# Routing of attention output to experts: one piece per pair of batches, or small steps beside attention blocks

## The chip, the cores and the metric

The kernel runs on one core of a Trainium2 chip. The metric is the device time of one execution in microseconds (us), lower is better. The executions came from several chips; a ratio is always taken between kernels that ran in the same rounds on the same chip. An execution counts as fast when it is within 1.5% of the fastest of its kernel in those rounds, otherwise as slow. Each also has a mean granted clock of TensorE (PE), 1.0 being full speed.

## The reference

The first half is chunked attention over 4 batches, 8 heads, 768 tokens and 64 dims. Its output, with the heads joined to 512 columns, goes into a mixture of 8 experts. A token takes its own best expert if it is the first of its batch or if its local gate is under 0.5; otherwise it keeps the expert of the token before it, so a batch is a chain.

```python
for b in range(B):
    prev_e = -1
    for s in range(S):
        fresh_e = int(np.argmax(logits[b, s]))
        if s == 0 or local_gate[b, s] < 0.5:
            e = fresh_e
        else:
            e = prev_e if prev_e >= 0 else fresh_e
        prev_e = e
        p = softmax(logits[b, s])
        h = np.maximum(x[b, s] @ w1[e], 0.0)
        out[b, s] = p[e] * (h @ w2[e])
```

## The kernel before

Attention runs in 32 blocks of 96 queries (NB = 32, 8 to a batch, NR = 16 to a pair of batches, HALF = 4). Each block has, as the trace counts them, 16 score matmuls, 16 value matmuls, four transposes ("turn") and, every fourth block, a group of gate logits. After each pair of batches the rows are routed: VectorE (DVE) picks experts and runs the chain as scans, the place of every row is worked out, GpSimd (POOL) scatters the rows of x to DRAM, grouped by expert, and gathers them back as tiles of 128. The first pair is routed while the second pair's attention runs, and the first five tiles ("early") come from it alone. Weights come in 8 pieces of 512 KB a tile, so 16 for the first two tiles, issued by SyncE (SP), which issues the loads of q and k too; v is issued by ScalarE (ACT). Loads run three blocks ahead.

```python
xp = ctx.enter_context(tc.tile_pool(name="xp", bufs=3))     # x of one batch: 3 for 4 batches
ld = inner.enter_context(tc.tile_pool(name="ld", bufs=AHEAD + 1))   # AHEAD = 3

def load(n):
    qt = ld.tile([P, HP, QB], F32, name="qt")
    nc.sync.dma_start(qt, q[n])
    kt = ld.tile([P, HP, P], F32, name="kt")
    nc.sync.dma_start(kt, k[n])
    vt = ld.tile([P, H, VW], F32, name="vt")
    nc.scalar.dma_start(vt, v[n])
    return qt, kt, vt

# ... scores, values, turned, logits cut ...

def route_ranks():                       # after route_picks over all 16 blocks
    onehot = sm.tile([PE2, S], F32, name="onehot")
    for half in range(2):
        # 4 transposes of pick into c_ps, a copy of its second part to stays
        nc.vector.tensor_tensor_scan(
            onehot[:, HQ * half:HQ * half + HQ], stays, c_ps[0:PE2].rearrange("p j n -> p (j n)"),
            onehot[:, HQ - 1:HQ] if half else 0.0, ALU.mult, ALU.add)
    rank = sm.tile([PE2, S], F32, name="rank")
    nc.vector.tensor_tensor_scan(rank, onehot, onehot, 0.0, ALU.add, ALU.max)
    # ... count kept ...

def route_rows(r, x, ex, tot, rank):
    # transposes of rank to r_ps, row numbers and probabilities on DVE, then for b, n:
    ins = nc.gpsimd.indirect_dma_start(            # 16 scatters a pair
        out=x_dram[:, :], out_offset=bass.IndirectOffsetOnAxis(ap=row[:, i:i + 1], axis=0),
        in_=x[b][0:QB, n].bitcast(I32), in_offset=None).ins

for n in range(NB):
    b, j = divmod(n, NQB)
    if j == 0:
        xs[b] = xp.tile([P, NQB, XW], F32, name="x")
    ahead = begin(n + 1) if n + 1 < NB else None   # scores of the next block, load n + 4
    make_values(*begun, n, xs[b][0:QB, j])
    begun = ahead
    if n > 0:
        turn(n - 1)                                # transposes, every fourth time the logits
    if n == NR:
        held["picks"] = route_picks(lts.pop(0))
    if n == NR + 1:
        held["ranks"] = route_ranks()
    if n == NR + 2:
        route_places(*held["ranks"])
    if n == NR + 3:
        route_rows(0, (xs.pop(0), xs.pop(1)), *held["picks"], held["ranks"][1])
    if n == NR + 4:
        early, done = plan_early()
    if n == NR + 6:
        early_xs = [gathered(early, i, (0,)) for i in range(EARLY)]
        # ... the pieces of the first two tiles' weights ...
    if n >= NR + 6:
        next(pieces)                               # one weight piece a block
for _ in pieces:
    pass
turn(NB - 1)
# ... then the experts: per tile 64 matmuls h_ps, 16 matmuls y_ps ...
```

## Time and profile before

| | kernel before |
|---|---|
| time of its first three executions | 558.06, 570.56, 573.6 us |
| profiled execution | 557.94 us, span 556.1 us, mean clock 0.947 |
| PE at half clock before 200 us of the span | 87.31 to 128.27 and 141.92 to 145.33, 44.4 us |
| first expert matmul | 140.63 us |
| rest of the span | 415.5 us |

In each profile quoted below that isn't from the chip described under C, the span minus the start of the first expert matmul is 414.2 to 417.0 us.

The page's row of engines (busy us, share of the span, instructions) says who is busy:

```profile
PE 531.4 (96%) x3614; PEld 406.4 (73%) x3614; DVE 88.0 (16%) x323; ACT 111.8 (20%) x224; POOL 90.8 (16%) x112
```

PE is the bound; DVE and POOL have much room.

### The profile page before, as it was taken

Reading aid. Unit: us, or ns where it says so; the run is one execution under the profiler, and the core shown is the slowest. Engines: PE = TensorE matmul, PEld = TensorE weight load, DVE = VectorE, ACT = ScalarE, POOL = GpSimd, SP = SyncE. Lnnn points to the kernel's source line nnn. Section 1 sums busy time; section 2 is a strip of 40 time slices with the busy share of each in tenths; the row PEclk is TensorE's granted clock in tenths of the full one; section 3 lists DMA queues with packets and bytes.
Section 4 is the critical chain, followed back from the end, with each engine's and each line's share of the span. In section 5 each row is a group of like instructions: output and inputs, shape, how many; then the busy total and the mean of one; then the engine's idle time right before and its main releaser. Section 6 shows DMA issues by size and latency. Waiting matters only on the chain.

```text
span 556.1 us, 9356 instructions
## 1 busy us (share of the span) xinstructions
PE 531.4 (96%) x3614; PEld 406.4 (73%) x3614; DVE 88.0 (16%) x323; ACT 111.8 (20%) x224; POOL 90.8 (16%) x112
## 2 busy tenths in 40 slices
PE   8999999998999999999999999999999999999970
PEld 5888889896877777777777777777777777766640
DVE  4333474123333000000000000000000100000000
ACT  3555553233110111111111111111111111101010
POOL 2000017310027321111111111112222111000000
PEclk9999996558899999999999999999999999999995
DMA  8777769995889999888989898889999998880000
GB/s 299 241 212 215 214 205 292 354 354 225 321 323 352 362 406 353 334 328 323 326 324 325 328 332 324 318 323 339 343 345 335 342 330 325 316 322 26 21 7 3
DMA packets 52761, 158.00 MB, mean 284 GB/s; under 512 B 7707, under 2 KB 11805, under 8 KB 52704
## 3 DMA queue, kind: packets, MB, share of 16 engines
q1 hardware_dynamic: 40320, 127.94, 64.1%
q0 software_dynamic: 6720, 20.78, 9.8%
q10 hardware_dynamic: 5664, 8.54, 5.1%
q8 instruction: 33, 0.54, 0.4%
q14 instruction: 24, 0.20, 0.1%
HBM read 144.62 MB, written 13.40 MB: 284 GB/s over the span
## 4 chain that ended last, share of the span: by engine, by line
PE 87%; issue 6%; DMA 2%; DVE 1%; ACT 0%; POOL 0%; POOLq 0%; DVEq 0%; ACTq 0%
PE h_ps L619 31%; PE y_ps L629 30%; PE o_ps L236 10%; PE s_ps L224 7%; DMA out_dram<-y,to 2%; PE xt_ps L279 2%; PE g_ps L606 2%; PE lt_ps L288 1%; PE l_ps L294 1%; PE z_ps L124 1%; DVE rank L348 0%; PE c_ps L341 0%; DVE x L239 0%; DVE onehot L344 0%; POOL out_dram L632 0%
## 5 line engine op out<-in xcount | busy, mean ns | idle before, releaser
L619 PEld LDWEIGHTS h_ps<-gxt,w_sb 128*128 128x128 f32 x1728 | 198.5, 193 | 14.2 <-issue 9.8
L619 PE MATMUL h_ps<-gxt,w_sb 128*128 128x128 f32 x1728 | 200.1, 277 | 3.3 <-DVE gxt L608 2.5
L629 PE MATMUL y_ps<-w_sb,ht 128*128 128x512 f32 x432 | 189.9, 592 | 0.0
L629 PEld LDWEIGHTS y_ps<-w_sb,ht 128*128 128x128 f32 x432 | 80.0, 190 | 90.4 <-issue 89.4
L632 POOL DMA_INDIRECT out_dram<-y,to x27 | 27.4, 1015 | 336.0 <-ACT y L631 320.9
L621 ACT ACTIVATE ht<-h_ps 128x512 f32<-128x512 f32 x54 | 32.2, 597 | 165.4 <-PE h_ps L619 165.4
L236 PE MATMUL o_ps<-vt,pt 128*96 128x65 f32 x512 | 60.3, 275 | 0.3 <-ACT pt L229 0.3
L236 PEld LDWEIGHTS o_ps<-vt,pt 128*96 128x96 f32 x512 | 54.5, 187 | 4.3 <-issue 1.7
L631 ACT ACTIVATE y<-y_ps,xs 128x512 f32<-128x512 f32 x24 | 16.5, 687 | 160.9 <-PE y_ps L629 154.2
L224 PE MATMUL s_ps<-qt,kt 64*128 64x96 f32 x512 | 46.7, 316 | 0.0
L224 PEld LDWEIGHTS s_ps<-qt,kt 64*128 64x128 f32 x512 | 39.2, 217 | 10.1 <-issue 7.0
L384 POOL DMA_INDIRECT x_dram<-x,row x32 | 29.5, 921 | 89.4 <-DVE x L379 80.2
L610 DVE TENSOR_TENSOR to<-xs,past_late 128x1 int32<-128x1 f32 x19 | 3.0, 160 | 236.0 <-DMA xs<-x_dram,rows_late 236.0
L608 DVE COPY gxt<-g_ps 128x512 f32<-128x512 f32 x27 | 18.6, 688 | 92.8 <-PE g_ps L606 92.8
L229 ACT ACTIVATE pt<-s_ps,mask_mid 128x256 f32<-128x256 f32 x72 | 29.0, 472 | 15.0 <-PE s_ps L224 14.7
L239 DVE TENSOR_TENSOR x<-o_ps,rinvs 96x256 f32<-96x256 f32 x64 | 26.8, 418 | 1.7
L280 ACT COPY xt<-xt_ps 128x384 f32<-128x384 f32 x32 | 15.3, 477 | 34.6 <-PE xt_ps L279 34.6
L238 DVE RECIPROCAL rinvs<-o_ps 96x4 f32<-96x4 f32 x64 | 11.4, 177 | 65.1 <-PE o_ps L236 64.1
L496 POOL DMA_INDIRECT xs<-x_dram,rows_late x19 | 18.3, 963 | 12.5 <-DMA x_dram<-x,row 7.1
L279 PE MATMUL xt_ps<-ident,x 96*128 96x96 f32 x128 | 18.5, 274 | 0.3 <-DVE x L239 0.3
L279 PEld LDWEIGHTS xt_ps<-ident,x 96*128 96x128 f32 x128 | 14.7, 167 | 0.5 <-issue 0.5
L606 PE MATMUL g_ps<-ident,xs 128*128 128x128 f32 x96 | 14.6, 273 | 0.0
(168 smaller groups left out, 131.1 us busy)
## 6 DMA issues: line engine op xcount, KB each, us to landing
w_sb<-in_w_dram SPq DMA_DIRECT2D x216, 512.0 KB, 6.7
vt<-in_v_dram ACTq DMA_DIRECT2D x32, 260.0 KB, 3.6
kt<-in_k_dram SPq DMA_DIRECT2D x32, 256.0 KB, 3.6
qt<-in_q_dram SPq DMA_DIRECT2D x32, 192.0 KB, 3.3
x_dram<-x,row POOLq DMA_INDIRECT x32, 7.8
out_dram<-y,to POOLq DMA_INDIRECT x27, 7.9
xs<-x_dram,rows_late POOLq DMA_INDIRECT x19, 7.8
x<-x_dram,rows_late POOLq DMA_INDIRECT x7, 8.1
```

What stands on the lines that cost most here:

```text
L224: nc.tensor.matmul(st[:, u, a], lhsT=kt[h, a], rhs=qt[h, a], start=True, stop=True)
L229: nc.scalar.activation(pt[:, :, :, c], st[:, :, :, c], ACT.Exp, bias=m[:, g:g + 1], scale=SCALE)
L236: nc.tensor.matmul(o_ps[:, a], lhsT=pt[:, u, a], rhs=vt[:, 2 * a + u], start=True, stop=True)
L239: nc.vector.tensor_tensor(x[:, 0:D].rearrange("p (a u d) -> p u a d", u=2, d=DH)[:, u], o_ps[:, :, 0:DH], rinv.to_broadcast([QB, HP, DH]), ...
L279: nc.tensor.transpose(xt_ps[:, kk], x[:, P * kk:P * kk + P], identity=ident[:QB, :QB])
L384: ins = nc.gpsimd.indirect_dma_start(out=x_dram[:, :], out_offset=bass.IndirectOffsetOnAxis(ap=row[:, i:i + 1], axis=0), in_=x[b][0:QB, n] ...
L606: nc.tensor.transpose(g_ps[:, kk], xs[:, P * kk:P * kk + P], identity=ident)
L608: nc.vector.tensor_copy(xt, g_ps)
L619: nc.tensor.matmul(h_ps[:, m], lhsT=w1_sb[:, kk, P * (g + m):P * (g + m) + P], rhs=xt[:, kk], start=(kk == 0), stop=(kk == DK - 1))
L621: nc.scalar.activation(ht[:, g:g + 4], h_ps, ACT.Relu)
L629: nc.tensor.matmul(y_ps, lhsT=ht[:, m], rhs=w2_sb[:, m], start=(m == 0), stop=(m == FK - 1))
L632: return nc.gpsimd.indirect_dma_start(out=out, out_offset=bass.IndirectOffsetOnAxis(ap=to, axis=0), in_=y, in_offset=None, bounds_check=NT ...
```

## The change

The change takes the routing apart into steps that each go with one attention block. Picks are made for four blocks at a time, the scans work on half a batch at a time, and the first half is done while the second half's attention runs. The rows go two blocks later (NR + 5, not NR + 3), the plan and gathers three. The weight pieces begin four blocks later (NR + 10, not NR + 6). The x pool gets a fourth buffer, and the planner's scratch is laid into a dead tile to make room for it.

```diff
-    xp = ctx.enter_context(tc.tile_pool(name="xp", bufs=3))
+    xp = ctx.enter_context(tc.tile_pool(name="xp", bufs=B))
@@ picks (cut): the same operations on HALF blocks of one batch
-    def route_picks(lt):
+    def route_picks(r, b, half):
+        js = slice(HALF * half, HALF * half + HALF)
+        lg, ex = r["lt"][:, js, b], r["ex"][:, js, b]
@@ scans (cut)
-    def route_ranks():
+    def route_experts(r, half):        # transposes and the scan of one half
+    def route_ranks(r, half):
+        of_half = slice(HQ * half, HQ * half + HQ)
+        nc.vector.tensor_tensor_scan(rank[:, of_half], onehot[:, of_half], onehot[:, of_half],
+                                     rank[:, HQ - 1:HQ] if half else 0.0, ALU.add, ALU.max)
@@ planner
+        scratch = sm.tile([P, S], F32, name=f"scratch_{name}", tag="onehot")
@@ order
+        for b in range(PAIR):
+            for half in range(2):
+                at(NQB * b + HALF * half + HALF + PAIR - b, route_picks, b, half)
+        at(NQB + HALF + 2, route_experts, 0)
+        at(NQB + HALF + 3, route_ranks, 0)
+        at(NR + 2, route_experts, 1)
+        at(NR + 3, route_ranks, 1)
+        at(NR + 4, route_places)
@@ main loop
-        if n == NR + 3:
-            route_rows(0, (xs.pop(0), xs.pop(1)), *held["picks"], held["ranks"][1])
-        if n == NR + 4:
+        if n == NR + 5:
+            route_rows(0, routes[0], (xs.pop(0), xs.pop(1)))
+        if n == NR + 7:
             early, done = plan_early()
-        if n == NR + 6:
+        if n == NR + 9:
             early_xs = [gathered(early, i, (0,)) for i in range(EARLY)]
-        if n >= NR + 6:
+        if n >= NR + 10:
             next(pieces)
```

Cut from the diff: token numbers are copied into x by POOL at a batch's start, and the second pair's steps are handed out around the first expert tiles.

## The prediction

> **What bounds the kernel now.** I read the page's 40 slices first, then a table of busy time by stage, then the chain that ended last, then single stretches. The slices show one thing that busy shares hide: TensorE (PE) is 90% busy almost everywhere, yet its granted clock falls to half from the seventh slice to the tenth.

> ```profile
> PE   8999999998999999999999999999999999999970
> PEclk9999996558899999999999999999999999999995
> ```

> A slice is 13.9 us, so this lies between 85 and 130 us, in the second half of the attention. By stage (columns: busy us of PE, PE weight load, DVE, ACT, POOL with instruction counts, then clock, DMA share, GB/s):

> ```profile
> 5.39:67.00 61.61, 61.35 (x721) 53.53 (x721) 21.13 (x76) 33.35 (x78) 0.00 (x0) 1.00 0.77 240
> 67.00:87.31 20.31, 19.66 (x222) 17.14 (x220) 14.19 (x59) 9.63 (x23) 4.62 (x5) 1.00 0.68 202
> 87.31:128.27 40.96, 40.96 (x270) 35.37 (x269) 10.06 (x42) 11.99 (x28) 14.79 (x16) 0.50 0.99 349
> 128.27:140.60 12.33, 9.91 (x110) 8.46 (x109) 5.72 (x20) 4.80 (x11) 0.00 (x0) 1.00 0.40 157
> 188.88:489.00 300.12, 300.12 (x1756) 221.28 (x1756) 15.78 (x41) 39.50 (x63) 46.24 (x47) 1.00 0.91 335
> ```

> The last row is the expert stage: PE without a gap at full clock, 14.45 us a tile. The change touches nothing there. The third row is what can be won: the same instructions take nearly twice as long, as the chain of waits shows for one block's scores:

> ```profile
> 60.16 1.06 PE s_ps L224 x16
> ...
> 89.23 1.96 PE s_ps L224 x16
> ```

> So up to 140.6 us the bound is PE at the clock it is granted. The DMA share of 0.99 in the third row is no bound: PE waits for no load of more than 0.2 us there. What starts the half clock? It falls at 87.31. Three stretches of 3.41 us, a regular one and two in the routing of the first two batches:

> ```profile
> 53.17:56.59 3.42, 3.42 (x45) 3.21 (x44) 1.40 (x6) 1.54 (x4) 0.00 (x0) 1.00 0.67 206
> 73.65:77.07 3.42, 2.86 (x34) 2.46 (x32) 3.42 (x7) 2.33 (x6) 0.00 (x0) 1.00 0.74 223
> 83.89:87.31 3.42, 3.42 (x41) 3.16 (x40) 1.76 (x15) 1.20 (x3) 2.67 (x3) 1.00 0.78 196
> ```

> [...] no gap between 10 and 87 us is over 1 us; thin work was enough. [...]

> **The change part by part.** The order of instructions in the built programs shows where the parts go.

> *Picks by four blocks.* Before, 14 DVE operations of 96x128, 3.3 us with evictions between (67.2 to 70.75). After, four sets of about 9 on a quarter of the columns, at some 0.17 us (the 16-column rows) 1.5 us each: 6 us instead of 3.3, but three of four sets lie beside earlier blocks. DVE is busy 21 of 62 us there, and a block has 3.36 us, of which evictions take 1.2. No cost.

> *Scans by halves.* The 1.75 us scan becomes two of about 0.9, the 1.0 us product two of 0.5; the first half goes five blocks earlier. The 0.6 us of PE gap goes.

> *Thin PE work apart.* The routing's small matmuls stay (c_ps 0.84, b_ps 0.18, r_ps 0.55, totals and plan about 1.1; 2.7 us), but the plan no longer meets logits in one window.

> *Clock.* Regular blocks take 13.45 us for four (scores at 40.90 and 54.35), 3.36 each. The half-clock row has 104 value and 112 score matmuls at 16 a block, 6.75 blocks: 22.7 us at full clock, so 18.3 lost. The row from 67 to 87.31 has five blocks, 16.8 us, 2.7 of routing, 0.8 of stall. Together 19.1 us to win.

> *Given back.* The rows of batches 0 and 1 are scattered by POOL, 16 times 1.215 us, and the gathers wait for all of them to land:

> ```profile
> 81.33 0.98 POOL L384 DMA_INDIRECT x_dram<-x,row  x1 [76.59 <-DVE x L379]
> ...
> 99.62 0.91 POOL L384 DMA_INDIRECT x_dram<-x,row  x1 [0.30 <-issue]
> 108.43 0.99 POOL L496 DMA_INDIRECT xs<-x_dram,rows_early  x1 [7.90 <-DVE rinvs L238]
> ```

> 27.1 us from first scatter to first gather, 6.6 more to land: hidden before, as experts began at 140.63. After, I lay the new order out at full-clock durations: the rows' transposes end near 82.5, the first scatter goes at 84, the first gather at 111, its rows land near 117.7. PE wants them near 115. So a new wait of about 3 us, in front of the last block's turn and logits. From the end of the first tile's transposes to the first expert matmul took 4.7 us (135.95 to 140.63): experts begin at 117.7 + 0.4 + 4.7 = 122.8, which is 17.8 us earlier. The first tile ran 9.01 us instead of 7.14 because the gap at 136 to 141 brought one more half-clock window; a longer gap may bring two: 1 us back. Sum: -17.8 + 1.0 = -16.8; 557.9 - 16.8 = 541 us.

> *Weights four blocks later.* In the old kernel the first pieces go at 88.8. In the new one they follow the loads of block 29, near 92, and the last fourteen go at once near 98.5: 7.3 MB at 350 to 400 GB/s is 20 us. The first tile's 4 MB are there by 110. Hidden. The token copies on POOL lie in its idle start.

> **The rivals.** *The clock falls anyway.* In the new order the rows' transposes (16 columns each) and the base product stand right behind a four-block logits group. Sliding a 3.413 us window over the order at full-clock durations, windows that begin just behind the wide logits matmuls hold 2,280 to 2,450 columns. 22% of the phases have a window under 2,450, against 42% for the old order laid out the same way, which has real stalls on top. With stalls I take 30% for a run. Then half clock from about 80 us to 115 to 140: 556 to 565 us. *PE was bound by loads.* Without half clock attention needs its 215 GB/s and the weights and scatters on top; the row at 0.99 shows 349 GB/s moving without waits, so I give this 3 to 5 us at most. *DVE becomes the bound:* it adds 3 us per pair over 50 us; unlikely. *Nothing moves,* because the gather wait eats it: it would have to be 16 us long; the chain above gives 3.

> **Range and chances.** Of the three times of before, 558.06 to 573.6, the profiled one was like the lowest. I read the others as runs in which the clock did not come back before the experts; that is a guess. A run that keeps its clock should take 537 to 547, one that loses it 556 to 565. With 70% for a run, the middle of several keeps it in somewhat over 75%. Prediction 542 us, range 536 to 561. Against 558 that is 2.9% less, against 570.56 5.0%. Chances: faster 0.77, same 0.21, slower 0.02.

> **What would show it.** Right: full clock without a break from 5 us to about 118; no 3.41 us stretch between 67 and 115 under 2,450 columns; first scatter near 84, first gather near 111, and PE waiting for it (the destination sums or the transposes of the first tile waiting on a DMA); first expert matmul near 123; 14.45 us a tile after that. Wrong: a half-clock row inside the attention, beginning behind the logits at about 78 to 82 us; or weights that land after 123; or a fall of the clock with over 2,600 columns in the window before it, which would refute the count as the cause.

## More of the kernel before

The view of waits from 60 to 140 us (engine, line, what it waited for, us in total, times, longest; L381, a copy of token numbers, is the first write to a batch's x):

```profile
DVE x L381 <- DMA x_dram<-x,row: 3.3, 1, 3.3
```

With three buffers for four batches, the fourth batch's x lies where the first batch's x was, and DVE waits until the first batch's rows have been scattered. The timeline of SP's queue (start, us, what was issued; L516 are weight pieces):

```profile
88.84 0.89 SPq L516 DMA_DIRECT2D w_sb<-in_w_dram  x2
91.22 0.34 SPq L128 DMA_DIRECT2D qt<-in_q_dram  x1
91.61 0.70 SPq L130 DMA_DIRECT2D kt<-in_k_dram  x1
```

Weight pieces stand in the same queue as q and k, ahead of loads that attention will need three blocks later.

## The result, and the profile after

| | before | after |
|---|---|---|
| executions of the same rounds | 558.06, 570.56, 573.6, 560.23 us | 552.52, 551.0, 552.52, 552.29 us |
| median | 565.39 us | 552.4 us |
| mean clock, profiled execution | 0.947 | 0.961 |
| half clock before 200 us | 44.4 us | 30.7 us, 108.04 to 138.76 |
| first scatter, first gather | 81.33, 108.43 us | 86.97, 113.90 us |
| first expert matmul | 140.63 us | 135.75 us |

The ratio of the fast runs is 0.987 (95% interval 0.983 to 0.992), which counts as the same at a margin of 2%. A ratio here is the mean time of one kernel's fast runs over that of the other's fast runs of the same rounds, so it is not quite the ratio of the medians. The time lies in the forecast range, but 10 us above the forecast, and the class is not the one given the best chance.

The 40 slices of the changed kernel, PE's busy share and granted clock:

```profile
PE   8999999788999999999999999999999999999970
PEclk9999999955999999999999999999999999999995
```

The clock holds through the routing and falls later, in the ninth slice; from the slice before it PE is no longer at 9. By stage (same columns as in the prediction):

```profile
66.00:87.00 21.00, 21.00 (x253) 18.80 (x252) 12.91 (x57) 11.10 (x28) 0.03 (x1) 1.00 0.65 197
87.00:109.00 22.00, 19.56 (x228) 17.31 (x224) 10.90 (x59) 10.45 (x26) 14.62 (x16) 0.98 0.98 318
109.00:139.00 30.00, 25.21 (x152) 21.60 (x153) 9.51 (x45) 6.20 (x15) 4.79 (x5) 0.50 0.90 346
```

The first row is the routing: PE is busy for 21.00 of 21.00 us at full clock. The new trouble is in the second and third rows. The chain of waits from 92 to 140 us names it (start, us, what):

```profile
95.77 15.74 DMA kt<-in_k_dram
111.51 0.14 issue
111.64 1.17 PE s_ps L224 x8
```

A load of k stood on the path for 15.74 us. The median load of k in this profile takes 2.9 us. The view of waits has the same from PE's side:

```profile
PE s_ps L224 <- DMA kt<-in_k_dram: 5.1, 1, 5.1
```

And SP's queue shows what was ahead of that load (L526 are weight pieces):

```profile
93.50 0.91 SPq L526 DMA_DIRECT2D w_sb<-in_w_dram  x2
95.38 0.34 SPq L128 DMA_DIRECT2D qt<-in_q_dram  x1
95.77 0.44 SPq L130 DMA_DIRECT2D kt<-in_k_dram  x1
98.97 0.33 SPq L128 DMA_DIRECT2D qt<-in_q_dram  x1
```

Two weight pieces of 512 KB are in front of the loads of the last two blocks. The scatters run at the same time:

```profile
86.97 0.99 POOL L393 DMA_INDIRECT x_dram<-x,row  x1 [81.69 <-DVE pick L327]
...
105.28 0.91 POOL L393 DMA_INDIRECT x_dram<-x,row  x1 [0.31 <-issue]
113.90 0.99 POOL L506 DMA_INDIRECT xs<-x_dram,rows_early  x1 [7.71 <-DMA x_dram<-x,row]
```

Three blocks of lead are 10.1 us at full clock (3 times 3.36), and k took 15.74. PE stood from 106.57 to 111.64 us, the clock fell at 108.04 and stayed at half until 138.76. From 90 to 112 us SP's queue, with weights, q and k, held 44.6% of the DMA engines' time and the scatters' queue 39.0%, and the k issued behind the two pieces landed after 15.74 us. In what order a DMA engine serves the two queues is not shown here.

The source says "four blocks later", but in the built program the first two pieces moved from ahead of the load of block 28 to ahead of the load of block 30. Versions with the weights' line moved two or three blocks further gave the same order on SP when built; they were not run. So the line in the source doesn't decide where these issues stand.

### The profile page after: what moved, and what is told of

Its sections match the earlier page's. It is cut to its first block, busy times and chain, and to the rows that moved or that the text cites.

```text
span 550.8 us, 9415 instructions
## 1 busy us (share of the span) xinstructions
PE 521.7 (95%) x3614; PEld 398.1 (72%) x3614; DVE 91.6 (17%) x369; ACT 112.3 (20%) x230; POOL 90.9 (17%) x116
## 4 chain that ended last, share of the span: by engine, by line
PE 85%; issue 6%; DMA 5%; ACT 0%; POOL 0%; DVE 0%; POOLq 0%; SPq 0%; DVEq 0%; ACTq 0%
PE h_ps L641 32%; PE y_ps L651 30%; PE o_ps L236 8%; PE s_ps L224 6%; DMA kt<-in_k_dram 3%; DMA out_dram<-y,to 2%; PE g_ps L628 2%; PE xt_ps L279 2%; PE lt_ps L288 1%; PE l_ps L294 1%; PE z_ps L124 1%; PE c_ps L334 0%; PE r_ps L379 0%; POOL out_dram L654 0%; ACT pt L229 0%
## 5 line engine op out<-in xcount | busy, mean ns | idle before, releaser
L236 PE MATMUL o_ps<-vt,pt 128*96 128x65 f32 x512 | 55.1, 262 | 0.4 <-ACT pt L229 0.4
L236 PEld LDWEIGHTS o_ps<-vt,pt 128*96 128x96 f32 x512 | 50.1, 175 | 3.4 <-ACT pt L229 0.6
L224 PE MATMUL s_ps<-qt,kt 64*128 64x96 f32 x512 | 41.8, 292 | 5.1 <-DMA kt<-in_k_dram 5.1
L224 PEld LDWEIGHTS s_ps<-qt,kt 64*128 64x128 f32 x512 | 34.9, 195 | 14.4 <-issue 11.5
L506 POOL DMA_INDIRECT xs<-x_dram,rows_late x19 | 18.3, 962 | 12.2 <-DMA x_dram<-x,row 6.8
L238 DVE RECIPROCAL rinvs<-o_ps 96x4 f32<-96x4 f32 x64 | 11.1, 175 | 50.3 <-PE o_ps L236 49.4
```

Of the source, the lines that this page charges most:

```text
L224: nc.tensor.matmul(st[:, u, a], lhsT=kt[h, a], rhs=qt[h, a], start=True, stop=True)
L236: nc.tensor.matmul(o_ps[:, a], lhsT=pt[:, u, a], rhs=vt[:, 2 * a + u], start=True, stop=True)
```

## The experiments

Five chips took part, A, B, C, D and E here. The kernel before had medians of 561.06, 594.48, 560.88, 559.88 and 561.83 us on them. B was in a slower condition throughout and is told apart below.

### A. Is it the load of k?

The first version, `after_wlast`, is the change with every weight piece held until the last load of k has been issued. All other engines keep their order of instructions.

```diff
+    last_load = [None]
-        nc.sync.dma_start(kt, k[n])
+        last_load[0] = nc.sync.dma_start(kt, k[n]).ins
-        if n >= NR + 10:
-            next(pieces)
-    for _ in pieces:
-        pass
+    with tc.issue_after(last_load[0]):
+        for _ in pieces:
+            pass
```

> The changed kernel with one thing altered: every expert weight piece is queued behind the last block's k load (before, two pieces stood ahead of the q and k loads of blocks 30 and 31). Instruction order on the four compute engines is identical. Theory 'two weight pieces ahead of the loads': k of block 30 lands in under 11 us instead of 15.7, PE waits for it less than 1 us instead of 5.1, no half clock between 87 and 116 us, first expert matmul at 122 to 126 us instead of 135.7, time 540 to 546 us, ratio to before 0.96 to 0.975. Rival 'the row scatters alone starve the loads': k still takes 13 us or more, PE waits 3 us or more, half clock from about 108, time 550 to 553. Rival 'weights now come too late': the first tile waits for a weight piece, time over 548 with full clock up to 116.

Measured on chip A: 547.08, 550.99, 547.48 us and one slow run of 567.09; ratio to the kernel before 0.979 (0.975 to 0.983). There is no wait for k. The scatters are still there, and the slowest load of k takes 10.3 us where it took 15.7: the pieces ahead of it make the difference. The clock row of its page and its longest wait of PE:

```profile
PEclk9999999995999999999999999999999999999995
123.14 1.12 PE L629 MATMUL g_ps<-ident,xs 128*128 128x128 f32 x4 [6.11 <-DMA xs<-x_dram,rows_early]
```

Full clock lasts to 120.15 us, half clock shrinks from 30.7 to 13.65 us, and the first expert matmul comes at 130.00, 5.75 us earlier than in the change. The next wait stands behind: 6.11 us for gathered rows. For that the expectation, experts at 122 to 126 us and a time of 540 to 546 us, was missed.

The second version, `after_qk4`, leaves the weights where the change has them and loads q and k four blocks ahead, v still three.

```diff
@@ load split into load and load_v, one more buffer for q and k, main loop likewise (cut)
-    loaded = {n: load(n) for n in range(AHEAD)}
+    for n in range(AHEAD + 1):
+        loaded[n] = load(n)              # q and k
+        if n < AHEAD:
+            loaded_v[n] = load_v(n)
```

> The changed kernel with q and k loaded four blocks ahead instead of three (v stays at three); the order on the four compute engines is identical, two weight pieces still stand ahead of the last block's loads. Theory 'a load that lands later than its lead': the lead grows from 10.1 to 13.5 us, so the wait for k shrinks from 5.1 us to under 2.5; if it goes under about 1 us the clock holds, and the time is 540 to 546; if not, 546 to 552. Rival 'the fall at 108 us has nothing to do with the load': half clock of about 30 us again and 551 to 553 whatever the wait.

Measured on A: 545.98, 547.57, 551.94 us, slow 569.24; ratio 0.979 (0.974 to 0.984). No wait for k, 13.65 us at half clock, and again a wait for gathered rows, 4.58 us. Two edits that have only the timely loads of q and k in common give the same gain, so the late k is the cause of that part. The change itself was not run in these rounds, and its interval (0.983 to 0.992) meets theirs, so it is the profiles that carry this comparison.

The change itself was run once more, on chip D, as `after_again`, with no edit.

> The change itself, on the chip of the others of this call. Theory: TensorE waits about 5 us for k in front of the scores of block 30 and the clock halves for about 30 us; ratio to the kernel before 0.983 to 0.992, runs of 550 to 553 us. Rival (the wait for k was that one execution's): no wait for k over 1 us, runs of 545 to 549 us as with the weights held back. On a chip with the stall at the scatters all are near 590 us and only the ratios among these four kernels count.

Measured: 551.6, 553.23, 552.24 us, slow 567.0; PE waited 3.81 us for k, 27.3 us were at half clock, the first expert matmul came at 133.52. The ratio to the kernel before is 0.993 with a wide interval (0.979 to 1.006), because that kernel was at 552.75 to 562.5 there. The wait for k comes back in another execution on another chip. `after_wlast_b` repeats the held-back weights on chip C, as a yardstick.

> The change with every weight piece behind the last load of k, again, as the yardstick of this chip. Theory: no wait for k over 1 us, ratio to the kernel before 0.974 to 0.984 as in its first run. Rival (the first run's gain was the chip's): 0.985 to 0.995, like the change itself.

Measured: 546.38, 546.16, 548.34 us and two slow runs, 567.3 and 565.66; ratio 0.980 (0.965 to 0.995). Its profile fell on a slow run, which is of use by itself. A stretch of 3.41 us in its routing, small steps and all (columns as in the prediction):

```profile
79.66:83.07 3.41, 3.41 (x43) 3.04 (x41) 2.41 (x10) 1.13 (x3) 0.00 (x0) 1.00 0.56 163
```

The clock fell at 83.07, at the end of this stretch, and 71.7 us at half clock followed. So the small steps do not keep the clock in each execution.

### B. What did the kernel before suffer from?

`before_again` is the kernel before with a profile of another execution, on chip A.

> The kernel before itself, to see whether its scatter of times is its clock. Theory: time and mean granted clock go together; every us at half clock costs about 0.45 us, so a run of 558 us shows 0.947 and one of 573 us about 0.92. Rival: runs of 558 and 573 us show the same mean clock within 0.005, and the difference is something else.

Measured: 562.82, 566.43, 563.14, 553.55, 565.45 and 560.78 us at mean clocks of 0.941, 0.931, 0.939, 0.964, 0.935 and 0.949: the time follows the clock. The 0.45 us of the expectation is an estimate from the prediction's 18.3 us lost in 40.96. In the profiled one (562.82, slow) the routing passed at full clock. Its waits from 78 to 140 us and its timeline of PE:

```profile
DVE x L381 <- DMA x_dram<-x,row: 7.2, 1, 7.2
100.28 1.03 PE L236 MATMUL o_ps<-vt,pt 128*96 128x65 f32 x5 [3.19 <-issue]
```

DVE waited 7.2 us for the x buffer, PE stood 3.19 us behind it, and the clock fell at 98.85 for 51.2 us. The view names only "issue" for PE's wait; that it stood behind DVE is read from the order: DVE's first eviction after its wait ended at 100.17, PE went on at 100.28. This is a second cause of the half clock, beside the routing. `before_wlast` is the kernel before with only the edit of `after_wlast`.

> The kernel before with its weight pieces queued behind the last k load, its routing untouched. Theory: there the loss is the clock that falls in the routing (half from about 87 us for 40 us), and loads have a lead of some 17 us at half clock, so moving the weights gives nothing: half clock again from 75 to 90 us on, PE waits under 1 us for loads, ratio 0.985 to 1.01. Rival 'the weights' place is the whole gain of the change': ratio 0.985 or less and the clock holds.

Measured: 573.22 (profiled, slow), 541.49, 550.77 and 553.91 us. The profiled one lost its clock in the routing, at 77.80 us, and was at half clock for 78.5 us. The expectation that this edit alone gives nothing in the kernel before did not foresee the 541.49; at a clock of 0.984 it was the first sign that the routing in one piece can run through undisturbed. Its runs scatter too much for a ratio. `before_xp4` is the kernel before with only the fourth x buffer (and the scratch that makes room).

```diff
-    xp = ctx.enter_context(tc.tile_pool(name="xp", bufs=3))
+    xp = ctx.enter_context(tc.tile_pool(name="xp", bufs=B))
```

> The kernel before with a fourth x buffer (and the planner's scratch laid into a dead tile to make room), nothing else. Theory (part of the gain is the buffer): the wait of VectorE for the rows scattered from x (3.3 and 7.2 us in two profiles of the kernel before) is gone, so one of the two causes of the half clock goes and the other, the routing passes in one piece, stays; ratio to the kernel before 0.98 to 0.995. Rival 1 (the small steps are all of it): ratio 0.995 to 1.005, and a fall of the clock in the routing in most executions. Rival 2 (the buffer is all of it): ratio like the change's, 0.987 or less. If VectorE and TensorE stall 8 to 14 us while the scatters are issued, as on the last chip, nothing of this can be read.

Measured on C: 556.97, 555.73, 556.86 us, slow 571.16; ratio 0.998 (0.982 to 1.014). The wait for x is gone, and PE's waits have this in its place:

```profile
PE s_ps L224 <- DMA kt<-in_k_dram: 3.8, 2, 2.1
```

The clock fell at 106.75, within these waits for k. Taking away one cause let the next one through. `after_xp3_b` is the reverse, the change with three x buffers, on C.

> The change with three x buffers, again, for a chip without the stall at the scatters. Theory (the fourth buffer counts): VectorE waits 3 to 8 us for rows scattered from x in front of the fourth batch's sums, TensorE behind it, and the time is 1 to 2% above the change's, so 0.99 to 1.00 of the kernel before. Rival (the buffer is worth nothing here): 0.985 to 0.99 of the kernel before, as the change.

Measured: 564.4, 565.0, 566.16, 566.43 us, ratio 1.015 (1.004 to 1.026), so slower than the kernel before. In its view of waits:

```profile
PE o_ps L236 <- DVE x L239: 7.6, 1, 7.6
DVE x L239 <- DMA x_dram<-x,row: 7.4, 1, 7.4
```

The steps without the buffer lose: the scatters begin later (86.97 us in the change, 81.33 in the kernel before), so the wait for the buffer is longer (7.4 us against 3.3 and 7.2 in two profiles of the kernel before), and 51.2 us at half clock follow. The line of one buffer is what separates the change from a loss. Its worth in the change is 0.987 against 1.015, two ratios from different rounds, so some 2.8% or 15 us.

### C. A chip in another condition

Four runs fell on chip B, where the kernel before took 586.88 to 598.01 us. `before_xp4_wlast` (the fourth x buffer and the held-back weights on the kernel before), `after_xp3` (the change with three x buffers), `wlast_g` (held-back weights, and the first tile's transposes kept behind the last logits) and `wlast_g_fill` (that and three useless matmuls of 128x512 in front of the transposes):

> The kernel before with four x buffers (the plan's scratch shared as in the changed kernel, to make room) and the weight pieces behind the last load; its routing still in large steps. It asks what the small steps themselves are worth. Theory 'the large steps make thin PE stretches, and whether one falls into a 3.413 us window is chance': no DVE wait on landing scatters at block 24, and two kinds of run: clock lost in the routing, 560 to 574, in at least two of six; clock kept, 538 to 546. Rival 'the x buffers and the place of the weights are the whole gain': all runs 538 to 546 and full clock until the experts.

> The changed kernel with three x buffers instead of four, as before. Batch 3's rows then have to wait until batch 0's scatters have landed. Theory: scatters begin near 87 us, so block 24's first eviction (near 88) waits for landings near 105: DVE waits 10 to 18 us, PE with it, half clock from about 95, 562 us or more. Rival 'the fourth buffer does not matter': 550 to 553 as the changed kernel.

> after_wlast with the first tile's transposes queued behind the last block's logits on TensorE; all else the same. In after_wlast PE stood 6.1 us at those transposes (waiting for the gathered rows), and the last turn and logits ran behind them at half clock, 6.9 us from landing to the first expert matmul (123.1 to 130.0). Theory 'the end of the attention waits for the gather, not for work': the first expert matmul comes 2 to 4 us earlier, near 126 to 128, ratio to before 0.965 to 0.976 in fast runs. Rival 'it is bound by the chain of turn, logits and copies anyway': no change, 130 and 547.

> wlast_g with three useless matmuls of 128x512 zeros (0.86 us each at full clock) between the last logits and the first tile's transposes. Theory 'the clock follows the activity of PE': they fill the wait for the gather, so that the half-clock stretch at the start of the experts is gone or at most 7 us (13.65 in after_wlast), and the time is 1 to 4 us below wlast_g although more is computed. Rival 'the clock falls for another reason': half clock as in wlast_g, time equal or up to 2.5 us longer.

Measured, ratios to the kernel before: 0.996 (0.986 to 1.006), 0.992 (0.984 to 1.000), 0.996 (0.989 to 1.002) and 0.991 (0.983 to 0.999). None of the questions is answered by these. In all four profiles DVE stands for 10 to 16 us in the early plan while POOL issues scatters, as the waits of `before_xp4_wlast` show:

```profile
DVE sums_early L455 <- remote: 16.1, 1, 16.1
PE xt_ps L281 <- DVE done L478: 14.0, 1, 14.0
```

PE stands 6.0 to 14.0 us behind it. Every version is at half clock for 72 to 82 us before 200 us, but in each the clock had fallen, at 83.23 to 94.37 us, before that stand of PE began; the stand did not start it. What the profile calls "remote" there stays open; in the profiles of the other chips the same copy waits 0.76 to 2.52 us, for a matmul. Three of the four kernels were run again on other chips, as `after_xp3_b` above and `wlast_g_fill_b` and `before_xp4_wlast_b` below; `wlast_g`, the held-back transposes without the useless matmuls, was not, so what these transposes do alone is not known.

### D. The wait for gathered rows

`wlast_g_fill_b` on chip C asks whether filling PE's time keeps the clock.

```diff
+        with tc.issue_after(last_l[0]):          # behind the last logits
+            f_ps = xps.tile([P, 512], F32, name="f_ps", tag="xps")
+            for _ in range(FILL):                # 3
+                last_l[0] = nc.tensor.matmul(f_ps, lhsT=zeros[:, 0:P], rhs=zeros, start=True, stop=True).ins
```

> The change with every weight piece behind the last load of k, with the first expert tile's transposes kept behind the last logits and three useless full matmuls between them, again, for a chip without the stall. Theory (what is left of the half clock at the end of attention is set off by TensorE idling for the gathered rows, and filled time keeps the clock): full clock from the start to the experts, or half clock for 7 us or less, against 13.65 in the version without the filler; ratio to the kernel before 0.96 to 0.975. Rival (the gathered rows come when they come): TensorE waits 5 to 6 us for them all the same, half clock 10 to 14 us, ratio 0.977 to 0.985.

Measured: 547.86, 547.06, 545.6, 549.9 us, ratio 0.982 (0.970 to 0.994): half clock 10.2 instead of 13.65 us, the first expert matmul at 129.28. Nothing is gained, but not as the rival said: PE did not wait for rows. Those of the first tile had landed by 122.32, when DVE used them, and PE came to their transposes only at 126.53, behind the useless matmuls, which took 5.13 us from 121.56, 1.71 each at half clock. The clock had fallen at 119.40, before these, with no gap of PE over 1 us in front; so the wait for rows is not all that sets off the half clock at the end of the attention. `wlast_early`, on chip D, does the last routing steps (ranks of the second half, places, rows, plan, gathers) one block earlier, on top of the held-back weights.

```diff
-        at(NR + 3, route_ranks, 1)
-        at(NR + 4, route_places)
+        at(NR + 2, route_ranks, 1)
+        at(NR + 3, route_places)
-        if n == NR + 5:                          # rows; plan and gathers likewise
+        if n == NR + 4:
```

> The change with every weight piece behind the last load, and the last steps of the first routing (the second half's ranks, the places, the rows with the scatters, the plan and the gathers) one attention block, about 3.4 us, earlier. Theory (the wait for gathered rows is set by when the scatters begin): first scatter about 2.5 to 3.4 us earlier than 87.9 us, gathers at about 113.5 us and not 116.8, TensorE's wait for them 3 us and not 6.1; first expert matmul 3 us earlier, runs of 543 to 545 us, if the clock doesn't fall in the routing. Rival (the landing of the scatters, slowed by other transfers, sets it): the gathers begin at 116 us or later, the wait stays 5 to 6 us, runs of 546 to 549 us.

Measured: 543.36, 543.18, 543.43, 542.65 us, ratio 0.976 (0.966 to 0.985), no slow run in four. Its first scatter, first gather and PE's wait for the rows:

```profile
85.50 0.99 POOL L395 DMA_INDIRECT x_dram<-x,row  x1 [80.20 <-DVE first L325]
...
113.43 0.99 POOL L508 DMA_INDIRECT xs<-x_dram,rows_early  x1 [8.70 <-DVE pick L327]
119.84 0.81 PE L629 MATMUL g_ps<-ident,xs 128*128 128x128 f32 x4 [2.93 <-DMA xs<-x_dram,rows_early]
```

Scatters 2.4 us earlier than in `after_wlast` (87.91), gathers 3.4 earlier (116.79), a wait of 2.93 for 6.11, the first expert matmul at 126.40 for 130.00. The wait is set by when the scatters begin. `best0` adds the filler, with four matmuls, to this.

> wlast_early with the first expert tile's transposes kept behind the last logits and four useless full matmuls between them. Theory: full clock up to the experts or half clock for 7 us or less, first expert matmul at 124 to 127 us, runs of 540 to 544 us, ratio to the kernel before 0.96 to 0.975. Rival (as in the version with the filler and the later scatters): half clock 10 us, first expert matmul at 128 to 130 us, 545 to 548 us.

Measured: 543.86, 542.95, 544.6, 544.6 us, ratio 0.977. Half clock falls to 6.8 us, but the first expert matmul comes at 127.98, since the useless matmuls took 5.50 us in front of the held-back transposes, which began at 126.60 where they had begun at 119.84. The filler is worth nothing here either.

### E. What are the small steps themselves worth?

`before_xp4_wlast_b`, on chip D, is the kernel before, routing in one piece, with the fourth x buffer and the held-back weights.

> The kernel before with a fourth x buffer and every weight piece behind the last load of k, routing still in one piece a batch pair: what differs from the version after_wlast is the small steps and the later places of the routing. Theory (the small steps are what spares the fall of the clock in the routing): of its executions a third to two thirds fall at 70 to 90 us and run 565 to 573 us, the others 541 to 551 us; with small steps about a third fell (4 of 13 so far). Rival 1 (the small steps do nothing): the share of falls and the times are those of after_wlast. Rival 2 (they cost, as the scatters come later): its executions without a fall are 3 to 8 us faster than those of after_wlast, 539 to 544 us.

Measured: 540.16, 539.95, 540.59 us and a slow run of 558.31; ratio of the fast runs 0.970 (0.957 to 0.984). The first scatter, first gather and first expert matmul of its timeline:

```profile
82.31 0.98 POOL L386 DMA_INDIRECT x_dram<-x,row  x1 [77.56 <-DVE x L381]
...
108.12 0.99 POOL L499 DMA_INDIRECT xs<-x_dram,rows_early  x1 [6.59 <-DVE rinvs L240]
122.97 9.01 PE L621 MATMUL h_ps<-gxt,w_sb 128*128 128x128 f32 x64 [0.93 <-PE l_ps L296]
```

Full clock to 123.37 us, no wait for rows, experts from 122.97: what the forecast promised of the small steps (122.8), reached without them. To rule out the chips, the versions with and without steps ran together on chip E for five rounds, as `steps_5` (the kernel of `after_wlast`) and `nosteps_5`.

> With the small steps, the fourth x buffer and the weights behind the last load of k, five rounds. Theory (the steps cost because the scatters begin some 5.6 us later): fast runs of 546 to 548 us, about 6 us above those of nosteps_5; TensorE waits 5 to 6 us for gathered rows. Rival (the difference was the chips'): both versions within 2 us of each other.

> Routing in one piece, with the fourth x buffer and the weights behind the last load of k, five rounds. Theory: fast runs of 540 to 542 us, no wait for gathered rows. A rival to the change's whole intent (the small steps spare falls of the clock in the routing): more executions over 556 us here than in steps_5. If the shares differ by no more than two of six, they can't be told apart.

Measured with steps: 546.65, 546.49, 545.61, 544.9, 546.38, 546.74 us, ratio 0.973 (0.968 to 0.978), a wait of 5.40 us for rows, experts from 129.16. Without steps: two fast runs, 539.17 and 540.37, and four slow ones of 564.97, 572.81, 570.62 and 565.69 at clocks of 0.918 to 0.932. The profiled fast run without steps has no wait for rows, experts from 122.32 and this clock row:

```profile
PEclk9999999998999999999999999999999999999995
```

So in fast runs the small steps cost some 6 us (546.1 in the mean against 539.8), because they begin the scatters 6.1 us later (87.77 against 81.65). In return fewer executions lost their clock: none of six against four of six here. Over all chips but B, 3 of 15 executions of this kernel with steps took over 556 us, against 5 of 10 without. The slow ones of `nosteps_5` have no profile. Two of them, at 0.918 and 0.921, have the clock of slow runs whose profiles show a fall in the routing (0.918 and 0.923); where the other two, at 0.932 and 0.931, lost theirs is not known. That the small steps spare falls in the routing is therefore suggested, not shown. The numbers of executions are small, and the share of losses may differ from chip to chip.

The version to keep is `wlast_early`: 543.27 us in the median with four runs within 0.8 us, faster than both kernels (the fast runs of the change in the same rounds took 551.6 to 553.23 us); its interval (0.966 to 0.985) is not wholly under 0.98. Routing in one piece with the two small edits is the fastest when it keeps its clock, and the most uneven.

## Why the prediction was wrong

The table sets out the profiled executions. "Wait" is PE's longest in front of the experts.

| version | half clock before 200 us | wait of PE | first expert matmul |
|---|---|---|---|
| before | 44.4 us | none over 1 us | 140.63 us |
| before, again | 51.2 | 3.19, behind the x buffer | 144.43 |
| before, fourth x buffer | 34.1 | 2.08 and 1.72, k | 138.27 |
| the change | 30.7 | 5.07, k | 135.75 |
| the change, weights last | 13.65 | 6.11, rows | 130.00 |
| the same, steps a block earlier | 10.2 | 2.93, rows | 126.40 |
| before, fourth buffer, weights last | 3.4 | none over 1 us | 122.97 |
| forecast for the change | none in attention | 3, rows | 122.8 |

**Failed: "Weights four blocks later" ... "Hidden."** This step asked only when the weights themselves would land. It didn't ask what they stand in front of. The pieces stand ahead of q and k in one queue, and the lead of three blocks shrinks when the clock is full: mostly at half clock, the kernel before issued its loads of q at 85.47, 91.22, 96.57 and 104.01 us, three blocks in 18.5 us, and at full clock three blocks take 10.1. Its own load of k behind the first two pieces (issued at 91.61) took 12.0 us, which 18.5 us hid and 10.1 would not have. So the gain expected of the clock took away the slack that hid the load. The rival "PE was bound by loads" named this, but was put at "3 to 5 us at most": the bare wait, 5.07 us, was about that, but the half clock that it set off was not counted. Holding the weights back brings the experts 5.75 us forward (135.75 to 130.00).

**Mis-sized: the new wait "of about 3 us" for gathered rows.** It measured 6.11 and 5.40 us once k was out of the way. Of this, the scatters begin at 87.91 and not at 84: the rows' transposes ended 1.4 us later than laid out (83.86 against 82.5, in the change's profile), and the few small DVE operations behind them stand between evictions of the running block, so the first scatter came 3.1 us after the transposes and not 1.5. The forecast let the clock hold through this wait; it fell to half for 13.65 us. From the start of the first tile's transposes to the first expert matmul took 6.86 us instead of 5.1. These two terms make up the remaining 7.2 us (122.8 to 130.00): the first tile's transposes began 5.4 us later (123.14 against 117.7), and 1.8 us were lost behind them.

**Half right: one cause of the half clock.** "What starts the half clock?" was answered from the single profiled execution, where the clock did fall in the routing. There were three causes behind one another: thin work in the routing (fall at 87.31 us in the kernel before; what in it decides is open, see below), the x buffer (fall at 98.85 in `before_again`; a line of the wait view that the prediction never read, and a line of the diff it never weighed), and k behind the weights (fall at 108.04 in the change). In the kernel before, removing the second alone gave 0.998. With the second and third removed, routing in one piece kept its clock in five of ten executions.

**Failed too: the count of columns.** Its number, about 2,450 columns in a window, does not hold. Counting the part of each matmul that lies within the window, the kernel before fell after about 2,310 and `after_wlast_b` after about 2,270, but `before_xp4` kept its clock through about 2,140 and 2,250. The prediction's own sign of being wrong, a fall with over 2,600 columns in the window before it, came as well: `before_again` fell at 98.85 after a window with about 3,770, in which PE was busy for 1.65 of 3.41 us. The second of the windows that `before_xp4` came through, with PE busy throughout like those two that fell:

```profile
86.27:89.69 3.42, 3.42 (x38) 3.10 (x36) 2.20 (x18) 1.71 (x5) 2.70 (x3) 1.00 0.83 273
```

What separates a thin window that costs the clock from one that does not stays open.

**Right.** The second half's scans no longer stall PE (21.00 busy of 21.00 us), DVE did not become the bound, the experts' part is unchanged (415.0 us against 415.5), and 14.45 us a tile came as forecast. That the experts started at 122.97 and 122.32 us in the versions with routing in one piece, near the forecast of 122.8, is luck: there the first tile's transposes began at 116.74 and 116.09 with no wait for rows and 6.2 us lay behind them, where the forecast had 117.7 after a wait and 5.1.

## What to carry to other kernels

When a kernel runs below its granted speed, ask what each hidden transfer's slack will be once the stage runs at full speed (three blocks took 18.5 us mostly at half clock and take 10.1 at full), and list what stands ahead of it in its queue: a bulk load that is itself in time may still delay a small one that isn't (a load of k took 15.74 us behind two weight pieces, and the slowest took 10.3 with the pieces held back). Read every wait in the stage in question, from more than one execution, before naming one cause, since removing the first shows the second (with the wait for x gone, PE waited 2.08 and 1.72 us for k in `before_xp4`). And weigh every line of a diff: here one buffer (0.987 against 1.015) and the place of a load (experts at 130.00 us, not 135.75) outweighed the restructuring that the change was named for.

## What these runs leave open

- What sets off a fall of the clock. It fell after a gap of PE of 2.08 us (at 106.75 us in `before_xp4`), and at the end of windows in which PE had no gap (about 2,310 and 2,270 streamed columns, at 87.31 us in the kernel before and at 83.07 in `after_wlast_b`). These runs yield no measure for thin work.
- What brings the full clock back. In the profiles of both kernels the clock is 1.00 or 0.50 alone, in stretches of 81.92, 40.96, 13.65 and 3.41 us before and of 102.40 and 30.72 us after, whole multiples of 3.413 us. Half clock lasted 30.7 us in the change with PE busy for most of it (25.21 of 30.00 us), and 40.96 us in the kernel before with PE busy for all of it.
- How late a small load comes behind bulk ones in general. In the one case here a 256 KB load behind two 512 KB pieces and beside 16 scatters took 15.74 us against a median of 2.9; with the pieces held back and the scatters still there the slowest took 10.3. Other sizes were not run.
- What the stall of chip B is: DVE held up 10 to 16 us in one small copy while POOL issued scatters, in every version profiled there, and 594.48 us for a kernel that took about 561 elsewhere.
